# Three moves in VectorE's order: the first cosine pieces, the parameter block and chunk 2's nb

## The chip, the cores and the metric

The kernel runs on one core of one Trainium2 chip. The metric is the device time of one execution in microseconds (us). The engines are TensorE (PE, matrix products; PEld is its weight load), VectorE (DVE), ScalarE (ACT), GpSimd (POOL) and SyncE (SP), which here issues most DMAs.

## The reference

The input x has 2048 rows of 512. With xn the layer norm of x over its rows (mean removed, divided by the square root of variance plus 1e-5), the result is x + A(xn) + B(xn):

```python
def _A_ref(x, Lambda_re, Lambda_im, B_re, B_im, C_re, C_im, log_dt, Dskip):
    Lam = Lambda_re + 1j * Lambda_im
    dt = jnp.exp(log_dt)
    Lam_bar = jnp.exp(dt * Lam)
    B_bar = ((Lam_bar - 1.0) / Lam)[:, None] * Bmat
    Bu = jnp.einsum("bld,pd->blp", x + 0j, B_bar)
    for t in range(L):
        h = Lam_bar[None, :] * h + Bu[:, t, :]
        ...
    return 2.0 * jnp.einsum("blp,dp->bld", hseq, Cmat).real + x * Dskip[None, None, :]

def _B_ref(x, w_gate, w_up, w_down):
    return (_silu(x @ w_gate) * (x @ w_up)) @ w_down
```

A is a diagonal state space model with 512 complex states. B is a gated feed-forward layer with 1376 inner columns. Inputs and output are bf16.

## The kernel before

The 2048 rows are four chunks (c = 0 to 3) of 512 columns of time, and each chunk is four tiles of 128 rows. For each chunk the kernel goes through these stages.

- **Layer norm.** `ln_stats` (L201, L202) takes mean and variance of a tile on VectorE. `ln_rstd` adds eps on VectorE (ve, L209) and raises to -0.5 on GpSimd (rstd, L210). Chunk 1's tiles are then normed on VectorE (L218); those of chunks 2 and 3 on ScalarE (L223), which needs nb = -mean × rstd from VectorE (`ln_nb`, L213). After each tile SP issues a transposing DMA (`xT_dma`, L249) into xnT, from which all matrix products read. Chunk 3 is normed into xn_end, the others in place in xall.
- **B projection.** `bproj_tile` (L370) makes eight PSUM banks of 128 × 512 per chunk, which ScalarE copies to u (L372).
- **State recurrence.** A complex recurrence with decay r and angle w is turned into a real one by rotating u with tables of cosine c16 and sine s16: six VectorE operations of 128 × 2048 (`rotation`, L380, L390, L394, called f1 to f6), eight scans (L412), a carry into the next chunk (L421 to L426), and six operations back, into wt. The product of wt with CF (C scaled by parameters) is `out_ssm` (L594). CF is made once by `c_ops`: ScalarE scales C into cm (L353), VectorE adds the other part (L356).
- **Feed-forward.** Gate and up products (L445) are evacuated by ScalarE (silu L464, copy L465) and multiplied on VectorE in pairs (L460). The last 96 columns go separately (L503, and `up_halves`, L492, which reads chunks 0 to 3 of xnT). Down products are L582 and L556.

The tables of two state quarters (q0 = 0, then q0 = 2) are made by `table_ops`, a list of ten pieces: for each q0 `turns` (L296, twice), `half(s16)` (L304, L305), `half(c16)` (L302, L304, L305), and two sines on ScalarE (L309). So `tables[0:5]` belongs to q0 = 0 and `tables[5:10]` to q0 = 2. These halves live in tiles called pm, of which there are three; the rotations use the same three. `params_turns` makes the angles; `params_sin` is two small sines on ScalarE (L324, L325); `params_b` is sixteen small VectorE operations (L321 to L342) that give the factors of CF.

The order of the work is a list by hand, without a scheduler. Matrix products are issued in program order; between them `pump(us)` takes pieces of side work from one list, `backlog`, as long as the time credited to it allows (each piece has a written cost in us), and `need(tag)` empties it until no piece of that tag is left. A piece that ScalarE executes is thus put in ScalarE's queue wherever the list has come to. Every engine executes its own queue in order. Chunk 2's `ln_rest` has the statistics of four tiles and ve in its first list, and nb and the four norms in its second; `spread` deals the second list and chunk 3's two lists out alternately with the pieces of chunk 0's recurrence.

Of the kernel before, what the change touches and what calls it, by code (L numbers as in the profile page):

```python
# [23 lines left out]
def kernel(  # L24
# [262 lines left out]
    def table_ops():  # L287

        ops = []
        for q0 in range(0, NQ, 2):  # L290
            box = {}

            def turns(q0=q0, box=box):
                box["tt"] = ssm.tile([128, 2, CW], F32, name="pm", bufs=3)
                for qq in range(2):
                    V.tensor_scalar(out=box["tt"][:, qq, :], in0=jidx[:], scalar1=ws2[:, 0, q0 + qq:q0 + qq + 1],  # L296
                                    scalar2=None, op0=ALU.mult)

            def half(dst, shift, q0=q0, box=box):
                tt = flat(box["tt"][:])  # L300
                if shift:
                    V.tensor_scalar(out=tt, in0=tt, scalar1=shift, scalar2=None, op0=ALU.add)  # L302
                km = box[shift] = ssm.tile([128, 2, CW], F32, name="pm", bufs=3)
                V.tensor_scalar(out=flat(km[:]), in0=tt, scalar1=MAGIC, scalar2=None, op0=ALU.add)  # L304
                V.scalar_tensor_tensor(out=flat(km[:]), in0=flat(km[:]), scalar=MAGIC, in1=tt,  # L305
                                       op0=ALU.subtract, op1=ALU.subtract)

            def sine(dst, shift, q0=q0, box=box):
                nc.scalar.activation(out=flat(dst[:, q0:q0 + 2, :]), in_=flat(box[shift][:]), func=ACT.Sin,  # L309
                                     scale=-TWO_PI_LO)  # L310

            ops += [(0.9, turns), (1.8, lambda half=half: half(s16, 0.0)),
                    (1.2, lambda half=half: half(c16, 0.25)), (0.6, lambda sine=sine: sine(s16, 0.0)),
                    (0.6, lambda sine=sine: sine(c16, 0.25))]
        return ops
# [300 lines left out]
    def queue(tag, ops, at=None):  # L616
        ops = [[op[0], op[1], op[2] if len(op) > 2 else None, tag] for op in ops]
        if at is None:
            backlog.extend(ops)
        else:  # L620
            backlog[at:at] = ops
# [40 lines left out]
    def ln_rest(c, on_act):  # L662
        ops = [(0.7, lambda n=n: ln_stats(n)) for n in range(c * TPC, (c + 1) * TPC)]
        def fin():
            ln_rstd(c * TPC, (c + 1) * TPC)
        def nbf():
            ln_nb(c * TPC, (c + 1) * TPC)
        ops += [(0.1, fin)]
        tail = [(0.1, nbf)] if on_act else []
        for n in range(c * TPC, (c + 1) * TPC):  # L670
            def one(n=n):
                (norm_act if on_act else norm_dve)(n)
                xT_dma(n)
            tail.append((0.05 if on_act else 0.35, one))
        return ops, tail
# [50 lines left out]
    head_mm(1, 2, 3, range(HK, KD), range(H))  # L726
    tables = table_ops()
    stats1, norm1 = ln_rest(1, False)
    queue("tables", [(1.0, params_turns)] + tables[:2])
    queue("ln1", stats1)  # L730
    queue("tables", tables[2:3])
    queue("ln1", norm1)
    queue("tables", tables[3:4] + [(0.1, params_sin)] + tables[4:])
    EARLY = 2 * H + 1
    EC = (TPC - 1) * 128
    for fi in range(H):
# [79 lines left out]
    def spread(ops, others, tag, tags):  # L816

        others = list(zip(others, tags))
        for op in ops:
            queue(tag, [op])  # L820
            if others:
                op, t = others.pop(0)
                queue(t, [op])
        for op, t in others:
            queue(t, [op])
# [6 lines left out]
    for part in range(2):  # L832
        for q in range(NQ):
# [2 lines left out]
            multiply(0 if q else 1)  # L836
    fwd0, back0 = ssm_ops(0)
    stats2, norm2 = ln_rest(2, True)
    queue("ssm0", fwd0[0:2] + [(1.5, params_b)] + fwd0[2:6])
    stats3, norm3 = ln_rest(3, True)  # L840
    queue("ln2", stats2)
    queue("ssm0", fwd0[6:8])
    spread(fwd0[8:] + back0, norm2 + stats3 + norm3, "ssm0",
           ["ln2"] * len(norm2) + ["ln3"] * (len(stats3) + len(norm3)))
    queue("cf", c_ops())
    load_late()
# [57 lines left out]
```

## Time and profile before

| | |
|---|---|
| median of 3 runs | 180.44 us (180.25 to 180.93) |
| profiled execution | 180.18 us, of which the span is 178.4 us |
| TensorE busy | 173.4 us (97%) |
| VectorE busy | 153.6 us (86%) |
| ScalarE busy | 95.1 us (53%) |
| GpSimd busy | 51.7 us (29%) |
| granted TensorE clock | 1.0 over the whole span |

The span goes from the first to the last instruction of the trace. Times in the timelines count from its start; each row has the start, the duration from the first start to the last end of the merged instructions, the engine, the line, the operation, output <- inputs, and in brackets the idle time before it with what ended that.

TensorE's work by time: the first tiles of chunk 0 to 18.3, its B projection to 25, more of its gate and up products, chunk 1's B projection from 31.2, chunk 1's gate and up from 38, chunk 2's B projection from 57.4, chunk 0's down product from 64.3, `up_halves` from 73.0, and chunk 0's C product from 75.5 on. Then chunks 2 and 3 follow in the same way until 175.5.

### The profile page before, as it was taken

To read this page: it belongs to the slowest core of one execution; us is meant where nothing else is said; L and a number is where in the kernel's file an instruction comes from. 1 tells how busy PE (TensorE), PEld (TensorE's weight loads), DVE (VectorE), ACT (ScalarE), POOL (GpSimd) and SP (SyncE) were. 2 spreads that over 40 slices of the span, in tenths; PEclk is the share of its full clock that TensorE was granted. 3 is DMA by queue.
4 is the path that set the end of the run, shared out by engine and by line. 5 is a ranking of instruction groups with operands and counts; after the bars stand their busy time and mean duration, and the time that the engine had idled before them with its cause. 6 is when DMAs were issued, how large, how long until landed. Compare 5 with 4: busy or idle time off the path is not lost.

```text
span 178.4 us, 2605 instructions
## 1 busy us (share of the span) xinstructions
PE 173.4 (97%) x955; PEld 83.4 (47%) x955; DVE 153.6 (86%) x232; ACT 95.1 (53%) x174; POOL 51.7 (29%) x85
## 2 busy tenths in 40 slices
PE   8999999999997999999999999999999999999993
PEld 3968544444443444344444444444444444444442
DVE  4876998899999976899999999999999999994033
ACT  3579697977199719942766662052866610001300
POOL 6050300000500040006999340049177240001410
PEclk9999999999999999999999999999999999999999
DMA  5999945996135002740000011019739800000652
GB/s 163 304 181 287 173 77 98 305 279 130 40 77 63 0 0 59 235 180 7 17 17 17 11 57 37 0 11 135 90 45 183 144 9 0 0 4 0 68 106 62
DMA packets 31292, 16.36 MB, mean 92 GB/s; under 512 B 20208, under 2 KB 31088, under 8 KB 31248
## 3 DMA queue, kind: packets, MB, share of 16 engines
q1 hardware_dynamic: 25232, 11.57, 28.1%
q0 software_dynamic: 5184, 4.07, 15.5%
q10 hardware_dynamic: 864, 0.56, 1.0%
q8 instruction: 7, 0.11, 0.3%
q14 instruction: 5, 0.04, 0.1%
HBM read 8.33 MB, written 5.24 MB: 76 GB/s over the span
## 4 chain that ended last, share of the span: by engine, by line
PE 61%; DVE 27%; DMA 4%; ACT 3%; POOL 2%; issue 1%; SPq 0%; DVEq 0%; POOLq 0%
PE ps L445 19%; PE ps L594 16%; PE ps L556 10%; DVE g L412 5%; PE ps L582 5%; DVE pm L380 4%; DVE stats L201 4%; PE ps L370 4%; DVE guT L460 3%; DMA xall<-in_A_x_dram 3%; PE ps L660 2%; DVE pm L305 2%; PE ps L545 2%; DMA xnT<-xn_end 1%; PE ps L683 1%
## 5 line engine op out<-in xcount | busy, mean ns | idle before, releaser
L445 PE MATMUL ps<-xnT,wu 128*128 128x512 bf16 (+1 forms) x148 | 36.7, 374 | 0.0
L445 PE MATMUL ps<-xnT,wg 128*128 128x512 bf16 (+1 forms) x148 | 36.6, 374 | 0.0
L370 PE MATMUL ps<-xnT,BT 128*128 128x512 bf16 x128 | 28.3, 379 | 0.9 <-DMA xnT<-xall 0.9
L412 DVE TENSOR_TENSOR_SCAN g<-r_t,car,u 128x512 bf16<-128x512 f32 x24 | 28.8, 1266 | 0.0
L594 PE MATMUL ps<-CF,wt 128*128 128x512 bf16 (+2 forms) x144 | 28.2, 356 | 0.0
L464 ACT ACTIVATE guT<-ps 128x512 bf16<-128x512 f32 (+1 forms) x40 | 23.6, 591 | 5.8 <-PE ps L445 5.5
L465 ACT CAST u<-ps 128x512 bf16<-128x512 f32 (+1 forms) x40 | 23.1, 577 | 6.5 <-PE ps L445 6.4
L607 ACT CAST res<-ps 128x512 bf16<-128x512 f32 x12 | 6.7, 590 | 36.0 <-PE ps L594 26.8
L445 PEld LDWEIGHTS <-wu 128*128 128x128 bf16 x148 | 14.4, 98 | 16.6
L445 PEld LDWEIGHTS <-wg 128*128 128x128 bf16 x148 | 14.4, 98 | 16.5
L185 POOL DMA_DIRECT2D gu_rows<-ul x36 | 17.7, 499 | 15.3 <-DVE ul L480 15.3
L372 ACT CAST u<-ps 128x512 bf16<-128x512 f32 x32 | 18.3, 590 | 5.5 <-PE ps L370 5.5
L608 POOL DMA_DIRECT2D out_dram<-res x12 | 10.5, 1222 | 34.8 <-ACT res L607 34.6
L594 PEld LDWEIGHTS <-wt 128*128 128x128 bf16 x144 | 13.2, 98 | 15.0 <-issue 0.8
L370 PEld LDWEIGHTS <-BT 128*128 128x128 bf16 x128 | 12.4, 98 | 16.1 <-issue 1.4
L210 POOL TENSOR_TENSOR rstd<-ve,neg_half 128x4 f32<-128x4 f32 x3 | 5.5, 1845 | 49.2 <-DVE ve L209 49.2
L582 PE MATMUL ps<-wd_sb,guT 128*128 128x512 bf16 x80 | 17.6, 380 | 0.0
L556 PE MATMUL ps<-wd_sb,guT 128*128 128x512 bf16 x80 | 17.4, 379 | 0.0
L460 DVE TENSOR_TENSOR guT<-guT,u 128x1024 bf16<-128x1024 bf16 x20 | 13.4, 680 | 0.0
L201 DVE BATCH_NORM_STATS2 stats<-xall 128x6 f32<-128x512 bf16 x14 | 9.5, 676 | 3.6 <-DMA xall<-in_A_x_dram 3.6
L582 PEld LDWEIGHTS <-guT 128*128 128x128 bf16 x80 | 7.8, 98 | 9.5
L556 PEld LDWEIGHTS <-guT 128*128 128x128 bf16 x80 | 7.8, 98 | 9.4
(120 smaller groups left out, 199.8 us busy)
## 6 DMA issues: line engine op xcount, KB each, us to landing
out_dram<-in_A_x_dram SPq DMA_DIRECT2D x1, 1536.0 KB, 7.0
out_dram<-res POOLq DMA_DIRECT2D x12, 128.0 KB, 3.3
out_dram<-xall POOLq DMA_DIRECT2D x3, 512.0 KB, 7.6
wd_sb<-in_B_w_down_dram SPq DMA_DIRECT2D x2, 640.0 KB, 8.4
xall<-in_A_x_dram SPq DMA_DIRECT2D x1, 1024.0 KB, 6.6
gu_rows<-ul POOLq DMA_DIRECT2D x36, 8.0 KB, 1.6
wg<-in_B_w_gate_dram SPq DMA_DIRECT2D x1, 512.0 KB, 5.0
wu<-in_B_w_up_dram SPq DMA_DIRECT2D x1, 512.0 KB, 5.9
```

What stands on the lines that cost most here:

```text
L185: nc.gpsimd.dma_start(out=gu_rows[c][i * RT:(i + 1) * RT, p, :], in_=product[p * RT:(p + 1) * RT, i * 128:(i + 1) * 128])
L201: nc.vector.bn_stats(out=stats[:, n, :], in_=xall[:, n, :])
L370: nc.tensor.matmul(ps[:], lhsT=BT[:, part, k, q * 128:(q + 1) * 128], rhs=xnT[:, k, c * CW:(c + 1) * CW], start=(k == 0), stop=(k == KD - 1))
L372: nc.scalar.copy(out=u_tiles[c][:, part, q, :], in_=ps[:])
L412: V.tensor_tensor_scan(out=g()[:, part, q, :], data0=r_t[:, q:q + 1].to_broadcast([128, CW]), data1=u_tiles[c][:, part, q, :], initial=ini ...
L445: nc.tensor.matmul(ps[:fs, lo:hi], lhsT=wslice(groups, fi, k), rhs=xnT[:, k, c * CW + lo:c * CW + hi], start=(k == 0), stop=(k == KD - 1))
L460: products.append(lambda: V.tensor_tensor(out=g, in0=g, in1=u, op=ALU.mult))
L464: nc.scalar.activation(out=gu_tile(c)[:, fi, 0:hi], in_=psg[:, 0:hi], func=ACT.Silu)
L465: nc.scalar.copy(out=u_tile(c, fi)[:, fi % 2, 0:hi], in_=psu[:, 0:hi])
L556: nc.tensor.matmul(o[:], lhsT=gu_tiles[k][:, fi, i * 128:(i + 1) * 128], rhs=wd_sb[:, fi, :], start=(fi == 0), stop=False)
L582: nc.tensor.matmul(o[:], lhsT=gu_tiles[c][:, fi, i * 128:(i + 1) * 128], rhs=wd_sb[:, fi, lo:hi], start=(fi == 0), stop=False)
L594: nc.tensor.matmul(o, lhsT=w_tiles[c][:, part, q, i * 128:(i + 1) * 128], rhs=CF[:, part, q, lo:hi], start=(fresh and part == 0 and q == 0 ...
```

## The change

It moves pieces within the written list. Ahead of chunk 1's statistics stands now also `half(c16)` of q0 = 0; the two first sines, `params_sin` and the `turns` of q0 = 2 come between those statistics and chunk 1's norms. `params_b` comes ahead of the first rotation piece of chunk 0 instead of behind its second. Ahead of the spread part stands one recurrence piece (a scan) instead of two, so that chunk 2's nb comes behind two scans instead of three. Nothing is computed otherwise.

```diff
-    queue("tables", [(1.0, params_turns)] + tables[:2])
+    queue("tables", [(1.0, params_turns)] + tables[:3])
     queue("ln1", stats1)
-    queue("tables", tables[2:3])
+    queue("tables", tables[3:4] + [(0.1, params_sin)] + tables[4:6])
     queue("ln1", norm1)
-    queue("tables", tables[3:4] + [(0.1, params_sin)] + tables[4:])
+    queue("tables", tables[6:])
...
-    queue("ssm0", fwd0[0:2] + [(1.5, params_b)] + fwd0[2:6])
+    queue("ssm0", [(1.5, params_b)] + fwd0[0:6])
     stats3, norm3 = ln_rest(3, True)
     queue("ln2", stats2)
-    queue("ssm0", fwd0[6:8])
-    spread(fwd0[8:] + back0, norm2 + stats3 + norm3, "ssm0",
+    queue("ssm0", fwd0[6:7])
+    spread(fwd0[7:] + back0, norm2 + stats3 + norm3, "ssm0",
```

In the built program TensorE's and SP's orders are the same as before. On VectorE the following stand elsewhere: `half(c16)` of q0 = 0 ahead of chunk 1's four statistics; two products (L460) ahead of the fourth of those statistics; the `turns` of q0 = 2 ahead of chunk 1's four norms; the parameter block ahead of the first rotation piece; chunk 2's nb behind two scans; chunk 3's ve ahead of two products (L460) and one back-rotation piece (L380) that it stood behind. On ScalarE the first two sines stand behind two and three copies (L372) of chunk 0's B projection instead of four and five, chunk 2's first norm stands one pair of feed-forward copies (L464 and L465) earlier, and chunk 3's first norm behind five copies of chunk 2's projection instead of six. On GpSimd the load of dsk_bc is issued behind the third power (L210) instead of the second.

## The prediction

> **What bounds the kernel now.** I read the page's head first, then TensorE's waits, then the timelines around the two waits that it has, and then went back along what released them. First two lines of the page, then two of TensorE's waits (line waiting <- what it waited for: us in total, times, longest):
>
> ```profile
> span 178.4 us, 2605 instructions
> PE 173.4 (97%) x955; PEld 83.4 (47%) x955; DVE 153.6 (86%) x232; ACT 95.1 (53%) x174; POOL 51.7 (29%) x85
> PE ps L370 <- DMA xnT<-xall: 0.9, 1, 0.9
> PE ps L492 <- DMA xnT<-xn_end: 0.3, 1, 0.3
> ```
>
> TensorE is the bound, and past its start it waits for data just twice, each time for the last transposed tile of a layer norm: chunk 2's (L370) and chunk 3's (L492). Nothing that VectorE does can shorten the span except through these two. TensorE's timeline tells what they cost:
>
> ```profile
> 54.53 1.03 PE L445 MATMUL ps<-xnT,wg 128*128 128x512 bf16 x4
> 55.40 1.03 PE L445 MATMUL ps<-xnT,wu 128*128 128x512 bf16 x4
> 57.37 7.07 PE L370 MATMUL ps<-xnT,BT 128*128 128x512 bf16 x32 [0.94 <-DMA xnT<-xall]
> ...
> 73.00 1.27 PE L492 MATMUL ps<-xnT,wu_last 128*64 128x512 bf16 x9
> 74.55 1.02 PE L492 MATMUL ps<-xnT,wu_last 128*64 128x512 bf16 x7 [0.28 <-DMA xnT<-xn_end]
> 75.50 0.39 PE L594 MATMUL ps<-CF,wt 128*128 128x512 bf16 x1
> ```
>
> Groups of four start 0.865 apart (54.53, 55.40), so L370 was due at 56.27 and came at 57.37: 1.10 lost, more than the 0.94 shown as idle, since a matmul's shown end lies behind the point where the next could start. L492's 16 matmuls run in pairs, 0.216 apart; the ninth began at 73.89, its partner waited until 74.55: 0.66 lost, not 0.28. The two are worth 1.76 by pitch, 1.22 by idle time. (Of this the Trainium skill, Perfetto Trace Analysis, Identifying the Most-Contended Engine, says that occupancy of matmuls measures headroom badly because they are pipelined; who sums idle time gets 1.22. The pitch in this trace bears the page out.)
>
> Where the wait comes from, in ScalarE's and VectorE's timelines:
>
> ```profile
> 48.92 0.81 ACT L223 ACTIVATE xall<-xall,nb,rstd 128x512 bf16<-128x512 bf16 x1 [3.90 <-DVE nb L213]
> 53.89 0.85 ACT L223 ACTIVATE xall<-xall,nb,rstd 128x512 bf16<-128x512 bf16 x1
> 66.88 0.81 ACT L223 ACTIVATE xn_end<-xall,nb,rstd 128x512 bf16<-128x512 bf16 x1 [3.54 <-DVE nb L213]
> ```
>
> ```profile
> 15.74 0.69 DVE L201 BATCH_NORM_STATS2 stats<-xall 128x6 f32<-128x512 bf16 x1 [1.66 <-DMA xall<-in_A_x_dram]
> ...
> 31.68 1.22 DVE L380 TENSOR_TENSOR pm<-u,c 128x2048 bf16<-128x2048 bf16 x1 [1.12 <-ACT c L309]
> ...
> 45.38 3.45 DVE L412 TENSOR_TENSOR_SCAN g<-r_t,u 128x512 bf16<-128x512 f32 x3
> 48.74 0.14 DVE L213 SCALAR_TENSOR_TENSOR nb<-mv,rstd 128x4 f32<-128x4 f32 x1
> ```
>
> ScalarE stands idle 3.90 and 3.54 for VectorE's nb; VectorE is busy from 31.68 to the first nb, but idle twice before: 1.66 for chunk 1's x, 1.12 for a cosine table. The change fills both holes and moves nb up one scan. Matrix work, its order and SP's order stay the same.
>
> **Part 1: the first cosine half ahead of chunk 1's statistics.** L302, L304, L305 took 2.59 (20.35 to the norm at 22.94). Now they start at 14.10, when the sine half's L305 has ended, and end the hole: statistics at 16.69, not 15.74. Three tiles at 0.80, two products (now ahead of the fourth tile, 1.20 together), the fourth tile: ve at 21.2 (was 19.06). GpSimd's power ended 2.01 behind ve: rstd at 23.2. VectorE comes there at 22.7, past a product (0.60) and the next two L296 (0.81, moved ahead of the norms), and waits 0.5. First norm 23.3 (was 22.94), so SP's four transposes start 0.33 later; the last is issued at 27.7 (was 27.4). At both waits TensorE started 2.55 to 2.60 behind the last issue, which gives 30.3; chunk 1's projection is due at 31.23. Cost nothing, by 0.9; were the power 0.2 longer (its longest ended 2.19 behind ve) still nothing. Behind the transposes on SP stand chunk 2's x, weights and the C matrices: 0.33 later too; x lands at about 36.2 (29.27 + 6.6 + 0.33) for a use at 39.6.
>
> ScalarE's first sines come after two L372 copies instead of four and five: 2.2 us of work while TensorE fills a bank per 0.865, so 2.5 of 8 banks. Nothing.
>
> **Part 2: parameters ahead of the first rotation.** With 2.59 taken out and the norms ended at 24.6, the last cosine L305 ends at 29.3 (was 30.56). ScalarE's sine of it then starts at 29.5, behind its copies, and ends at 30.6. Meanwhile the parameter block (34.56 to 36.59, 2.03) runs from 29.25 to 31.3, so the first rotation finds its table ready: the wait of 1.12 is gone. From the first rotation to chunk 2's statistics it was 41.98 - 31.68 = 10.30; less 2.03 it is 8.27: statistics at 39.6, 2.4 earlier.
>
> **Part 3: nb behind two scans.** Statistics to ve took 3.32: ve at 42.9. From ve to nb 3.44, less one scan of 1.12: nb at 45.25, 3.5 earlier. rstd was there 2.10 behind ve, so at 45.0: in time by 0.2. If it is late, nb waits on VectorE with the scans queued behind it. Here a row is open: GpSimd's power took 1.07 and 1.01 where VectorE ran single small operations, 1.76 to 1.93 beside two-input ones. At worst it begins only when the second scan has ended, and nb comes at 45.25 + 1.07 = 46.3; at best at 45.25. I take 45.25, since beside three scans it took 1.85. (The Trainium skill, SBUF — State Buffer, Who interferes with whom, has VectorE with two SBUF inputs and a GpSimd operation that reads SBUF shut each other out for a whole instruction; it would put nb at 46.3, and the power's 1.85 beside running scans does not settle it. The sum is the same by both.)
>
> ScalarE's norms (0.72 each) now stand with one pair of copies (0.95) behind each of the first two: 45.3 + 4 × 0.72 + 2 × 0.95 = 50.1 (was 54.7). xnT is there at 52.7; due at 56.27. The first wait is gone with 3.5 in hand: **-1.10**.
>
> **Part 4: chunk 3.** From chunk 2's statistics to the next ve was 64.45 - 41.98 = 22.47; two products and one L380 now come behind it (2.34): ve at 59.7. rstd 2.19 later: 61.9; VectorE reaches nb at 62.1 (was 66.68). ScalarE's first norm stands behind five copies of chunk 2's projection, which TensorE now starts at 56.27: done 61.4. So norms from 62.2; four norms, three copies (0.5) and two cm (0.61) between them end at 67.8, and xnT is there at 70.4. Due: 73.89 - 1.10 = 72.8. The second wait is gone, 2.4 in hand: **-0.66**.
>
> **What is late next.** Chunk 0's C product is the nearest: its seventh CF ended at about 75.9 for a matmul at 76.15. The cm and CF chain follows the norms: by the same pitches the seventh ends at 71.9 for a need at 74.4. Further on, chunk 1's wt ended at 103.0 for 117.6, gu_rows landed by 149 for 160.0, and chunk 3's wt ended at 161.9 for 168.4: all over 1.76. dsk_bc's load moves behind the third power on GpSimd, to about 62; its first reader is at 129. So the cover holds, and the sum is -1.76. The profiled execution took 180.18 (178.4 span and 1.8 around it) and would take 178.42; the median is 180.44, which makes **178.7**.
>
> **Rivals.** *The second wait takes back the first's gain.* Chunk 3's norms stand among copies paced by TensorE itself. For it: 74.55 is a date of its own, and if chunk 3 came no earlier the whole 1.76 would be lost (180.4); against it: ScalarE was idle 3.54 for nb alone. It begins to bite when nb comes after 64.5, 2.4 later than I have it; in between 178.7 to 180.4.
>
> *Chunk 1 pays.* If its norms are more than 0.9 later than worked out, TensorE stalls at 31.23. The longest power row adds 0.2, so a stall of more than 0.3 needs something not in the trace: 179.0.
>
> *Slower: PSUM fills behind ScalarE's norm.* Its first norm now stands one pair of tiles further up, behind the copy that ended at 43.23. If nb is late, ScalarE blocks; TensorE has eight banks, and the tile at 49.35 needs the first of them, whose copy lies 1.3 behind nb. So it decides from nb at 48.0; each us beyond costs one. At 49.8 the gain is gone, beyond 50.7 the kernel is over 0.9 slower: at 51.7, 182.4. Against it: even with nothing gained ahead, one scan less puts nb at 47.6, and with the power begun only behind the second scan 48.7, still faster. Only several delays that no row shows would do it.
>
> *The change does not do what it says.* In the built order the moved instructions stand as said, so only the sizes are open.
>
> **How the numbers follow.** Both waits gone: 0.80, at 178.7, alone 178.2 to 179.2 (the runs of before spread by 0.7). Second wait takes back some or all: 0.09, half still over 0.9 faster. Chunk 1 pays: 0.05, mostly small. PSUM fills or another loss: 0.06. 0.5% is 0.9 us, about what a measurement of this kernel can tell from no change. Faster 0.85, same 0.09, slower 0.06. The range goes from 178.1 to 179.8, which takes in half of the second rival and the first bound of chunk 1.
>
> **What would show it.** In the profile after: no wait of L370 or of L492 for a transpose; VectorE's 1.66 and 1.12 gone and about 0.5 new ahead of the chunk 1 norms; chunk 2's nb at 45 to 46, chunk 3's near 62; L370 of chunk 2 at 56.3, the first L594 at 73.7; span 176.6. Wrong if L370 at 31.23 is late, if nb waits over a microsecond, or if a new TensorE wait stands behind 56.

## The result and the profile after

The changed kernel takes 178.45 us (median of 6 runs, 178.35 to 178.62) against 180.41 for the kernel before on the same chip (180.17 to 180.96): a ratio of 0.9887, 95% interval 0.9869 to 0.9904, so 1.96 us less. Forecast were 178.7 and 1.76 less. The profiled execution took 178.62.

From the page of the changed kernel, its span, TensorE's row and the shares of the chain that ended last:

```profile
span 176.8 us, 2605 instructions
PE 173.1 (98%) x955; PEld 83.6 (47%) x955; DVE 153.6 (87%) x232; ACT 95.3 (54%) x174; POOL 50.7 (29%) x85
...
PE 98%; DVE 0%; issue 0%
```

The chain is now TensorE's almost from end to end; before, VectorE's rows held 27% of it. In TensorE's timeline neither wait is left:

```profile
55.61 1.03 PE L445 MATMUL ps<-xnT,wu 128*128 128x512 bf16 x4
56.48 7.07 PE L370 MATMUL ps<-xnT,BT 128*128 128x512 bf16 x32
...
72.11 1.92 PE L492 MATMUL ps<-xnT,wu_last 128*64 128x512 bf16 x16
73.96 7.08 PE L594 MATMUL ps<-CF,wt 128*128 128x512 bf16 x32
```

L370 starts one pitch (0.87) behind the group ahead of it, and L492 runs through in 1.85 up to L594, where it took 2.50 before. ScalarE's norms and VectorE's rows that led to the two waits:

```profile
45.18 0.81 ACT L223 ACTIVATE xall<-xall,nb,rstd 128x512 bf16<-128x512 bf16 x1 [1.73 <-DVE nb L213]
48.50 1.53 ACT L223 ACTIVATE xall<-xall,nb,rstd 128x512 bf16<-128x512 bf16 x2
62.09 0.81 ACT L223 ACTIVATE xn_end<-xall,nb,rstd 128x512 bf16<-128x512 bf16 x1 [0.52 <-DVE nb L213]
```

```profile
16.92 0.69 DVE L201 BATCH_NORM_STATS2 stats<-xall 128x6 f32<-128x512 bf16 x1
...
31.09 1.22 DVE L380 TENSOR_TENSOR pm<-u,c 128x2048 bf16<-128x2048 bf16 x1
...
42.76 2.33 DVE L412 TENSOR_TENSOR_SCAN g<-r_t,u 128x512 bf16<-128x512 f32 x2
45.01 0.14 DVE L213 SCALAR_TENSOR_TENSOR nb<-mv,rstd 128x4 f32<-128x4 f32 x1
```

No row of these VectorE lines has idle time in front of it: the holes of 1.66 and 1.12 are filled. ScalarE's waits for nb fell from 3.90 and 3.54 to 1.73 and 0.52.

The head of the kernel differs between profiles (chunk 0's B projection starts at 18.27 before and 18.49 after), so the two are best compared from there to the start of VectorE's last addition (L599), which waits for TensorE's last product: 157.20 before (18.27 to 175.47), 155.44 after (18.49 to 173.93). That is 1.76 less, the forecast sum. The 0.2 by which the medians differ from it is not in this pair of profiles.

### The profile page after: what moved, and what is told of

Read it like the earlier page. It is cut to its first block, busy times and chain, and to the rows that moved or that the text cites. A ratio compares the mean times of both kernels' runs of the same rounds, so it can differ in the third digit from the quotient of the medians.

```text
span 176.8 us, 2605 instructions
## 1 busy us (share of the span) xinstructions
PE 173.1 (98%) x955; PEld 83.6 (47%) x955; DVE 153.6 (87%) x232; ACT 95.3 (54%) x174; POOL 50.7 (29%) x85
## 4 chain that ended last, share of the span: by engine, by line
PE 98%; DVE 0%; issue 0%
PE ps L445 35%; PE ps L594 16%; PE ps L370 16%; PE ps L556 10%; PE ps L582 10%; PE ps L683 2%; PE ps L660 2%; PE ps L503 2%; PE ps L750 2%; PE ps L545 2%; PE ps L492 1%; PE ps L235 1%; DVE res L599 0%; PE ps L265 0%
## 5 line engine op out<-in xcount | busy, mean ns | idle before, releaser
L370 PE MATMUL ps<-xnT,BT 128*128 128x512 bf16 x128 | 28.3, 379 | 0.0
L594 PE MATMUL ps<-CF,wt 128*128 128x512 bf16 (+2 forms) x144 | 28.2, 356 | 0.0
L464 ACT ACTIVATE guT<-ps 128x512 bf16<-128x512 f32 (+1 forms) x40 | 23.5, 588 | 6.5 <-PE ps L445 6.0
L465 ACT CAST u<-ps 128x512 bf16<-128x512 f32 (+1 forms) x40 | 23.0, 575 | 6.9 <-PE ps L445 6.6
L372 ACT CAST u<-ps 128x512 bf16<-128x512 f32 x32 | 18.2, 587 | 6.0 <-PE ps L370 5.9
L594 PEld LDWEIGHTS <-wt 128*128 128x128 bf16 x144 | 13.2, 98 | 15.1 <-issue 0.8
L370 PEld LDWEIGHTS <-BT 128*128 128x128 bf16 x128 | 12.5, 98 | 14.9
L210 POOL TENSOR_TENSOR rstd<-ve,neg_half 128x4 f32<-128x4 f32 x3 | 4.6, 1534 | 44.9 <-DVE ve L209 44.9
L460 DVE TENSOR_TENSOR guT<-guT,u 128x1024 bf16<-128x1024 bf16 x20 | 13.4, 678 | 0.0
```

Of the source, the lines that this page charges most:

```text
L370: nc.tensor.matmul(ps[:], lhsT=BT[:, part, k, q * 128:(q + 1) * 128], rhs=xnT[:, k, c * CW:(c + 1) * CW], start=(k == 0), stop=(k == KD - 1))
L372: nc.scalar.copy(out=u_tiles[c][:, part, q, :], in_=ps[:])
L460: products.append(lambda: V.tensor_tensor(out=g, in0=g, in1=u, op=ALU.mult))
L464: nc.scalar.activation(out=gu_tile(c)[:, fi, 0:hi], in_=psg[:, 0:hi], func=ACT.Silu)
L465: nc.scalar.copy(out=u_tile(c, fi)[:, fi % 2, 0:hi], in_=psu[:, 0:hi])
L594: nc.tensor.matmul(o, lhsT=w_tiles[c][:, part, q, i * 128:(i + 1) * 128], rhs=CF[:, part, q, lo:hi], start=(fresh and part == 0 and q == 0 ...
```

## The experiments

The theory: VectorE's order counts only through TensorE's two waits; each costs what the date of the last transposed tile exceeds the date at which TensorE is due, in start-to-start time. Each run below is compared with runs of the kernel before on the same chip; all times are medians, and each kernel has one trace. "Lost" is read from its trace: the time between the starts of chunk 1's and chunk 3's B projection (L370) beyond the 67.57 of the changed kernel; before it is 69.32, so 1.75 lost.

| kernel | chunk 2's nb | lost in trace | time | before | difference |
|---|---|---|---|---|---|
| e1: parts 1 and 2 | 46.01 | 0.00 | 178.56 | 180.32 | -1.76 |
| e2: part 3 alone | 47.44 | 0.60 | 179.39 | 180.32 | -0.93 |
| e3: part 1 alone | 48.07 | 0.68 | 179.18 | 180.32 | -1.14 |
| e4: part 2 alone | 47.50 | 0.21 | 179.33 | 180.32 | -0.99 |
| e5: all, VectorE 1.1 later | 46.06 | 0.00 | 178.49 | 180.47 | -1.98 |
| e6: all, VectorE 3.4 later | 48.84 | 1.41 | 180.04 | 180.47 | -0.43 |
| e7: all, VectorE 4.5 later | 49.56 | 2.67 | 181.25 | 180.47 | +0.78 |
| e8: all, statistics beside the power | 45.67 | 0.00 | 178.49 | 180.47 | -1.98 |
| e9: e2, 12 VectorE instructions more | 48.01 | 0.60 | 180.12 | 180.70 | -0.58 |
| e10: e2, 16 ScalarE instructions more | 47.40 | 0.02 | 179.85 | 180.70 | -0.85 |
| e11: e2, 48 TensorE instructions more | 48.02 | 0.26 | 179.68 | 180.69 | -1.01 |

**e1, parts 1 and 2 without part 3.** From the changed kernel:

```diff
-    queue("ssm0", fwd0[6:7])
-    spread(fwd0[7:] + back0, norm2 + stats3 + norm3, "ssm0",
+    queue("ssm0", fwd0[6:8])
+    spread(fwd0[8:] + back0, norm2 + stats3 + norm3, "ssm0",
```

> The changed kernel with nb put back behind three scans and the spread list of before. Theory (the time depends on VectorE only through TensorE's two waits for transposed tiles): chunk 2's statistics as in the changed kernel at 39.4, nb2 at 46.1, xnT of chunk 2 ready 8 later at the latest, 54, due 56.5; nb3 at 64.1, xnT of chunk 3 ready 7.7 later, 71.8, due 73.0. Both waits stay away: 178.45, the time of the changed kernel. Rival (the gain follows how much earlier nb2 comes, here 2.6 of 3.7): 1.4 of the 1.96 gained, 179.0.

Measured 178.56, ratio 0.9910 (0.9894 to 0.9926), no wait in TensorE's list. Filling VectorE's holes is enough; nb behind three scans does no harm then. The rival, a gain in proportion to nb's date, falls: it gave 179.0.

**e2, part 3 alone.** From the kernel before, the same lines the other way round.

> The kernel before with only nb behind two scans and the new spread list. Theory: nothing gained ahead, nb2 at 47.6; chunk 2 ready at 55.1 to 55.8, due 56.27, and below the 48.0 from which PSUM would fill: the first wait is gone. Chunk 3's ve at 62.1, nb3 at 64.5, ready 8.3 later (as in the changed kernel), 72.8, due 72.8: the second wait is gone or up to 0.2. So 178.5 to 178.7, nearly all of the gain from the smallest of the three edits. Rival (gain in proportion to nb2, 1.1 of 3.7): 179.8.

Measured 179.39, ratio 0.9954 (0.9938 to 0.9970), 0.7 above what I expected. nb came at 47.44 (47.6 worked out) and chunk 3's wait is gone, but L370 still waits. TensorE's timeline, and the issue row of chunk 2's last transposed tile in the view of DMAs between 53.8 and 54.5 (count, and us to landing; above it the queue's packets, MB and share of the DMA engines):

```profile
55.60 1.03 PE L445 MATMUL ps<-xnT,wu 128*128 128x512 bf16 x4
57.01 1.24 PE L370 MATMUL ps<-xnT,BT 128*128 128x512 bf16 x5 [0.38 <-ACT guT L464]
```

```profile
q8 instruction: 1, 0.02, 11.4%
...
xnT<-xall SPq DMA_TRANSPOSE x1, 3.8
```

The tile was issued at 53.09 and landed 3.8 later, at 56.9, just ahead of 57.01; I had taken 2.4 to 2.6. The releaser named, a ScalarE silu (56.17 to 56.86), is put down by date alone. Taking the eight banks in turn, L370's first product gets the bank of the product that started at 49.49, and that bank was empty by 54.91, with this row of ScalarE's timeline:

```profile
54.26 0.65 ACT L464 ACTIVATE guT<-ps 128x512 bf16<-128x512 f32 x1
```

e9 to e11 go after the 3.8.

**e3 and e4, part 1 and part 2 alone.** From the kernel before, the hunk of the tables, or the line with `params_b`.

> The kernel before with only the table pieces moved (cosine half into the hole ahead of chunk 1's statistics). Theory: the hole of 1.66 is filled, but the first rotation still needs the second cosine's sine, which ends at 30.8, so it starts 0.85 earlier than before and not 1.66; nb2 at 47.9, chunk 2 ready at 56.4, due 56.3 to 56.5: first wait 0 to 0.2. nb3 at 65.8, ready 73.5, due 72.9: second wait costs about 0.6. 179.1, between 178.9 and 179.4. Rival (proportion, 0.85 of 3.7): 180.0.

> The kernel before with only the parameter block ahead of the first rotation. Theory: the block fills the wait of 1.12 for the sine and runs 0.9 past it; chunk 2's statistics 1.2 earlier, nb2 at 47.5, chunk 2 ready at 56.1, due 56.27: first wait gone. nb3 at 65.5, ready 73.2, due 72.8: second wait costs about 0.4. 178.9, between 178.6 and 179.2. Rival (proportion, 1.2 of 3.7): 179.8.

e3 took 179.18 (ratio 0.9944, 0.9930 to 0.9959), as expected; of its loss of 0.68, 0.11 is at L370 and the rest at `up_halves`:

```profile
72.40 1.27 PE L492 MATMUL ps<-xnT,wu_last 128*64 128x512 bf16 x9
73.86 1.02 PE L492 MATMUL ps<-xnT,wu_last 128*64 128x512 bf16 x7 [0.20 <-DMA xnT<-xn_end]
74.82 7.08 PE L594 MATMUL ps<-CF,wt 128*128 128x512 bf16 x32
```

72.40 to 74.82 is 2.42, 0.57 over the 1.85 without a wait, where the list shows 0.20 of idle time: again the loss by pitch is the true one. e4 lost 0.21 in its trace; its median of 179.33 (0.9946, 0.9931 to 0.9962) is 0.4 above what I expected and past its range. The profiled execution (178.92) was its fastest of six. The other five have no trace, so where they lost more is not known.

**e5, e6, e7, VectorE made late again.** The changed kernel with n = 1, 3 or 4 more VectorE operations ahead of chunk 2's statistics:

```diff
+    def idle_op():
+        t = ssm.tile([128, W], BF16, name="pm", bufs=3)
+        V.tensor_tensor(out=t[:], in0=flat(c16[:]), in1=flat(s16[:]), op=ALU.mult)
+    for _ in range(n):
+        queue("ln2", [(0.0, idle_op)])
     queue("ln2", stats2)
```

> The changed kernel with one more VectorE operation of 1.13 us (a product of the two tables into a spare tile, whose result nobody reads) ahead of chunk 2's statistics. Theory: nb2 at 46.1 and nb3 at 63.0; chunk 3 ready at 71.4, due 73.0: in hand, 178.45, no change against the changed kernel. Rival (VectorE's chain of work sets the end, as the chain of before named it): 1.13 later, 179.6.

> The same with three such operations, 3.4 us. Theory: nb2 at 48.4, just past the 48.2 from which PSUM fills: 0.2 lost; nb3 at 65.3, chunk 3 ready at 73.6, due 73.2: 0.4 lost. Together 0.6: 179.1. Rival (only the transposed tiles count, PSUM never fills): 0.65 lost all at chunk 3's wait, none at the tile of 49.6; TensorE's wait list tells the two apart. Rival (VectorE's chain sets the end): 181.8.

> The same with four, 4.5 us: VectorE as late as with nothing gained. Theory with PSUM: nb2 at 49.6, ScalarE's copy of the first blocked bank ends at 51.0, so TensorE waits 1.4 for ScalarE at the tile due at 49.6, ahead of any transposed tile; chunk 2 ready at 57.8, due 57.9 by then, no wait; nb3 at 66.4, chunk 3 ready at 74.8, due 74.4: 0.4. Together 1.8: 180.25, the time of before by another road. Without PSUM: chunk 2's wait 1.3 and chunk 3's 0.5 in its place, also 1.8; the wait list of TensorE decides.

e5: 178.49, ratio 0.9893 (0.9873 to 0.9913): 1.1 us more of VectorE's work in its busiest stretch cost nothing. e6: 180.04, ratio 0.9978 (0.9966 to 0.9989), 1.4 lost where 0.6 were expected. TensorE's rows with a wait in e6; by pitch they cost 0.36, 0.61 and 0.47, the last for the tile that landed at 58.18, 3.7 behind its issue:

```profile
50.36 1.02 PE L445 MATMUL ps<-xnT,wg 128*128 128x512 bf16 x4 [0.19 <-ACT guT L464]
54.41 1.02 PE L445 MATMUL ps<-xnT,wg 128*128 128x512 bf16 x4 [0.43 <-ACT guT L464]
58.32 7.07 PE L370 MATMUL ps<-xnT,BT 128*128 128x512 bf16 x32 [0.30 <-ACT guT L464]
```

e7: 181.25, ratio 1.0038 (1.0023 to 1.0053), slower than before, where 180.25 was expected. TensorE's and ScalarE's timelines of e7:

```profile
48.73 1.03 PE L445 MATMUL ps<-xnT,wu 128*128 128x512 bf16 x4
51.09 1.02 PE L445 MATMUL ps<-xnT,wg 128*128 128x512 bf16 x4 [1.33 <-ACT guT L464]
...
55.13 1.02 PE L445 MATMUL ps<-xnT,wg 128*128 128x512 bf16 x4 [0.44 <-ACT guT L464]
...
59.17 1.02 PE L370 MATMUL ps<-xnT,BT 128*128 128x512 bf16 x4 [0.42 <-DMA xnT<-xall]
```

```profile
49.74 0.81 ACT L223 ACTIVATE xall<-xall,nb,rstd 128x512 bf16<-128x512 bf16 x1 [6.27 <-DVE nb L213]
50.46 0.58 ACT L464 ACTIVATE guT<-ps 128x512 bf16<-128x512 f32 x1
```

ScalarE stands 6.27 for nb, then norms, then empties the first bank by 51.04, and TensorE starts at 51.09: PSUM was full. The first wait (by pitch 1.5, expected 1.4) sits where the slower rival had it. But there are two more: at 55.13 for the bank that ScalarE empties only behind its third and fourth norms (0.58 by pitch), and at 59.17 for chunk 2's last tile, again 3.8 behind its issue (0.59). Chunk 3's wait, expected at 0.4, did not come.

**e8, a statistics step beside the power.** In the changed kernel:

```diff
     queue("ln2", stats2)
+    queue("ln3", stats3[0:1])
```

(and the spread list takes `stats3[1:]`).

> The changed kernel with one statistics step of chunk 3 (one input) right behind chunk 2's ve, where a scan (two inputs) stood. Theory: GpSimd's power waits only for the end of the two-input VectorE operation that runs when it comes, and needs about 0.95 from there: beside the statistics it takes 1.0 to 1.1 instead of 1.85 and rstd is there 1.3 behind ve. Rival (any busy VectorE slows it): 1.8 again. By the rule that the one in progress holds the port for its whole length the scan that follows the statistics would also start late, by up to 0.4. The time stays at 178.45 by all of them, since nb still comes behind two scans and by 46.0.

178.49, ratio 0.9889 (0.9872 to 0.9906). GpSimd's timeline of the changed kernel, then that of e8 and its VectorE rows:

```profile
42.93 1.85 POOL L210 TENSOR_TENSOR rstd<-ve,neg_half 128x4 f32<-128x4 f32 x1 [19.85 <-DVE ve L209]
```

```profile
42.80 1.01 POOL L210 TENSOR_TENSOR rstd<-ve,neg_half 128x4 f32<-128x4 f32 x1 [19.85 <-DVE ve L209]
```

```profile
42.62 0.69 DVE L201 BATCH_NORM_STATS2 stats<-xall 128x6 f32<-128x512 bf16 x1
...
43.44 2.31 DVE L412 TENSOR_TENSOR_SCAN g<-r_t,u 128x512 bf16<-128x512 f32 x2
```

1.01 instead of 1.85, as expected. The first scan started while the power still ran (to 43.81), and the two took 2.31, as beside the power of the changed kernel (2.33).

**e9, e10, e11, whose instruction load is it?** In all profiles up to e8 a tile of chunk 2 that was issued 0.5 to 2 ahead of a 16 KB instruction load (queue q8) on the DMA engines took 3.5 to 4.3 to land; the others took 2.4 to 2.7. All three edits are made to e2:

```diff
 e9  +    for _ in range(12): nc.vector.memset(spare[:], 0.0)          # at VectorE's start
 e10 +    for _ in range(2): nc.scalar.copy(out=spare[:], in_=neg_half[:])   # behind each of 8 copies
 e11 -    dummy(8, CW)
 e11 +    dummy(32, 128)
```

> e2 (nb behind two scans, all else as before) with 12 tiny memsets of a spare tile more on VectorE in its idle stretch before 2.9 us. In e2 the last transposed tile of chunk 2 landed 3.8 behind its issue instead of 2.4, and an instruction load of 20 KB on the DMA engines (queue q8) ran at that time; so it did for the one slow transpose of every other profile. Theory: the load slows the transpose, and it comes when an engine's instruction stream has reached a certain place. If that engine is VectorE, 12 instructions more bring it some 7 us earlier, to about 47 instead of 54; the last tile then lands 2.4 behind its issue, at 55.5, the wait of L370 (0.61 by pitch) is gone, and the time is 178.7 instead of 179.4. Rival (ScalarE's stream calls it): the load stays at 54, nothing changes, 179.4. Rival (back-to-back transposes are slow here, load or no load): the load moves but the tile still takes 3.8, 179.4.

> e2 with 16 tiny copies to a spare tile more on ScalarE, two behind each copy of chunk 1's B projection, where it waits 0.28 for TensorE each time. If ScalarE's stream calls the instruction load, 16 instructions bring it from 54 to before the norms, about 43 to 47; the last transposed tile of chunk 2 lands 2.4 behind its issue, at about 55.6, L370 no longer waits and the time is 178.7. If VectorE's stream calls it, the load stays at 54, the tile takes 3.8 and the time is 179.4. If neither moves it, the load goes by time or by another engine. The tiny copies themselves fit into the gaps: no change by them.

> e2 with TensorE's eight warm-up matmuls of 512 columns cut into 32 of 128 columns, so with 48 instructions (weight loads and matmuls) more ahead of all its work. The seven instruction loads of 16 to 20 KB in each trace follow one another as TensorE gets through 256 instructions (the fifth comes 6.3 behind the start of chunk 3's B projection in every profile), so they should be TensorE's own. Then 48 instructions move each load earlier by 24 matmuls, 5.2 us where these have 512 columns: the third to 49 instead of 54, the fifth to 1.1 behind chunk 3's B projection's start. The last transposed tile of chunk 2 then has no load beside it and lands 2.4 behind its issue; L370's wait (0.61 by pitch) is gone: 178.7 instead of 179.4. Rival (the loads belong elsewhere, or the third only fills a hole in the transposes): the third stays 1.0 behind the issue of the last transpose, which takes 3.8; 179.4.

More instructions on VectorE or ScalarE left the load where it was (54.65 and 54.08; 54.12 in e2) and the tile at 3.7 and 3.8. That date alone says little, for in these three the load starts just as the tile ahead lands (0.08 to 0.13 before). The fifth load, which has no transpose near it, says more: it came 6.3 behind the start of chunk 3's B projection in e2, e9 and e10 alike, and 1.9 behind it in e11. With 48 more on TensorE the third load came at 45.95, and the fifth to seventh 3.6 to 5.1 earlier too, when TensorE had started about as many matmuls as in e2 (592, 718 and 839; 589, 711 and 839 in e2). The fourth came 1.1 later, which stays open. The last tile, issued at 53.66, then had no load beside it:

```profile
xnT<-xall SPq DMA_TRANSPOSE x1, 2.5
```

So the loads go by TensorE's progress, and the one trace in which the third was moved away has no slow tile. L370's wait for the tile was gone; 0.26 were lost at the product that in e7 waits at 55.13. e10 lost only 0.02 although its tile took 3.8: its TensorE ran 0.55 later than e2's with nb at the same date (47.40), so the tile that landed at 56.84 was just in time for L370 at 56.98. The medians of these three (ratios 0.9962, 0.9957 and 0.9951 for e9, e11 and e10, each about 0.002 either way) do not tell them from e2, and the expected 178.7 was not reached: in the traces their heads were 0.4 to 0.6 longer than e2's, and the medians lie another 0.5 to 0.7 above the traced executions. What the load costs is shown in the trace alone.

## Why the prediction was right

- **What bounds the kernel.** Right, and the step that carried the sum: 1.10 and 0.66 by pitch. The medians went by 1.96, the traces by 1.76, idle time would have given 1.22. The 0.2 between medians and traces is not explained. e5 shows that VectorE's own length does not count, though the chain of before ran through it.
- **Part 1.** Statistics came at 16.92 (16.69, and the head 0.2 later). The wait of 0.5 for rstd was 0.1, since the power took 1.38 and not 1.76 or more. Chunk 1's projection did not wait: its last tile landed at 30.45, 1.0 ahead of it (0.9 forecast). A reading was off without effect: TensorE started 2.53 to 2.60 behind the last issue at the two waits, not 2.55 to 2.60.
- **Part 2.** The first rotation came at 31.09 (31.3), chunk 2's statistics at 39.36 (39.6).
- **Part 3.** nb came at 45.01 (45.25), rstd in time by 0.2 as forecast, not 1.07 late. The last norm ended at 50.03 (50.1). The step "xnT is there at 52.7" was too early: SP issued the fourth tile at 50.64 and it took 3.9, so 54.6. In hand were 1.9, not 3.5. The kernel before has such a tile too, its third, which was issued at 52.72 and took 3.6; I had read only the last. That the forecast held all the same is owed to the margin, not to this step.
- **Part 4.** nb came at 61.91 (62.1), the last norm ended at 67.7 (67.8).
- **What is late next.** Nothing, as forecast; the six CF operations from 68.33 put the seventh at 71.7 (71.9).
- **The slower rival.** Its place was right and its price too low. I had it decide at nb of 48.0 and cost one us per us; e6 lost 1.41 at 48.84 and e7 2.67 at 49.56. Left out were the bank behind the third and fourth norms and the slow tile. The kernel is slower than before by 0.78 at 49.56 already, where I had some gain left until 49.8. At 45.01 the changed kernel stays clear, and e5 shows 1.1 more to be free.
- **The parts are not additive.** Part 1 and part 2 together give all of it; the three alone give 1.14, 0.99 and 0.93, 3.06 in sum, for a gain that ends at 1.96. e1 shows that part 3 is not needed beside parts 1 and 2; whether it could stand in for one of them was not run.

## What to carry to other kernels

Where one engine is the bound, list its waits first, price each by the start-to-start pitch around it, and work out for every moved piece the date at which that wait's releaser comes: the sum of those is all that a reordering elsewhere can give, and edits that each remove the same wait do not add. Work out the margin at the date as well, with every place at which the waiting engine's queue holds up another, since a blocked evacuation costs at each bank that it delays and not only at the first.

## What the runs showed of the hardware

- Instruction loads of 16 KB run on the DMA engines (seven in each trace). They go by TensorE's progress: the fifth to seventh moved with TensorE's count of matmuls (e11) and not with VectorE's or ScalarE's (e9, e10). A transposing DMA of chunk 2 issued 0.5 to 2 ahead of one landed 3.5 to 4.3 behind its issue instead of 2.4 to 2.7; when the load was moved away, all four took 2.4 to 2.5 (e11). Why it costs more than a microsecond, and why the third load comes 1.0 to 1.3 behind a transpose's issue in eleven of the thirteen traces, stays open.
- GpSimd's power of 128 × 4 took 1.01 beside a one-input VectorE operation (e8). Beside two-input ones it ended 0.8 to 0.9 behind the end of the operation in progress when it came (scan of the changed kernel: 43.98 to 44.78; L390 of before: 65.75 to 66.64), but 1.25 behind it in one place, beside two L460 in a row (before: 19.82 to 21.07). The Trainium skill (SBUF — State Buffer, Who interferes with whom) says that the later of the two is shut out for the whole instruction. For a power behind a VectorE operation the runs agree; but a scan that started while the power ran in e8 (43.44, the power until 43.81) was not held up (two scans in 2.31).
